# Another order of issue for the steps of a delta-rule attention and MLP-mixer kernel

## The chip, the cores and the metric

The kernel runs on one core of one Trainium2 chip. The metric is the device time of one execution in microseconds. Before the change the median of three runs is 701.34 us (700.79 to 702.61).

## What is computed

Two blocks follow each other. The first is a delta-rule recurrence over 768 positions for 4 batches of 8 heads of 48 features; the second is an MLP mixer on its output, 4 x 768 x 384, in float32:

```python
for t in range(S):
    kt, vt, bt = (k_n[:, :, t], v[:, :, t], beta[:, :, t, None])
    y[:, :, t] = np.einsum('bhd,bhde->bhe', q[:, :, t], state)
    v_old = np.einsum('bhde,bhd->bhe', state, kt)
    state = state + bt[:, :, :, None] * np.einsum('bhd,bhe->bhde', kt, vt - v_old)
...
xt = x.transpose(0, 2, 1)
h = np.maximum(xt @ w_tok1, 0.0) @ w_tok2
u = x + h.transpose(0, 2, 1)
h2 = np.maximum(u @ w_ch1, 0.0) @ w_ch2
return (u + h2).astype(np.float32)
```

k_n is k divided by its norm. The token weights are 768 x 256 and 256 x 768, the channel weights 384 x 1536 and 1536 x 384.

## The kernel before

The recurrence is computed in chunks of 64 positions, two to a unit u of 128; there are 24 units, six to a batch. Every piece of work is a Python generator, a job, that issues a few instructions and yields. One string, `order`, names the job whose next step is issued; "p0*3" means three steps of job p0. Nothing else sets the order. Each engine takes its instructions in the order in which the steps issue them, and the semaphores follow from the tiles that they share. So a step in the string stands at once in the queues of all the engines that it uses, and an instruction that waits holds those behind it on its engine.

The jobs, by the first letter of their names:

- k, v (lines 326 and 354): loads of k and q, and of v, for a unit, issued from SP's queue; v ends with a scaling on GpSimd.
- p (line 374): norms on ScalarE and VectorE, transposes of k and q into p_t and their copies, the product p_g of keys and queries (64x64 array tiles), its masking on VectorE (line 442), then the parts of the matrix that is to be inverted.
- i (line 531): the inversion of the unit triangular 32x32 blocks of a round of units, some thirty dependent pairs of VectorE instructions (lines 553 and 558). Rounds 0 and 1 (units 0 to 3, and 4 and 5) have a shorter way that works on 16x16 halves and stays in SBUF; later rounds go through DRAM (n_dram, w_dram).
- f, h, j (lines 514, 577 and 608): bring the inverses back, and join the halves with small matmuls (p_z and p_x, on 32x32 array tiles).
- r (lines 635 and 712): the recurrence, one step for each chunk of 64, 48 in all. Within a step of the first batch, VectorE subtracts (line 659), PE forms p_w, ScalarE copies it, PE forms p_s, and VectorE updates the state (line 688). The next chunk needs that state.
- m (line 880): the mixer of a batch: the token product p_1 (six steps), the second token product p_h (six steps, each added on VectorE), then the channel products p_c and p_o. From batch 1 on the channel products use seven products in the place of eight.
- w (lines 237 and 273): a piece of a weight matrix: a load, then rounding on ScalarE, VectorE and GpSimd. There are 34; s forms sums of weights, b loads beta.
- x, z, y and Y (lines 196 and 205): fillers. x multiplies a tile of zeros with itself, 128x128; z does so with 512 columns; y and Y issue four matmuls of 64x128. All write p_warm, which nothing reads, and wait for nothing but the zeros.

PE's matmuls in float32 show as two records each in the profile, transposes as one.

Of the kernel before, what the change touches and what calls it, by code (L numbers as in the profile page):

```python
# [23 lines left out]
def kernel(  # L24
# [1052 lines left out]
    r3*3 w14 p7 p8 p7 j2 p7 k10*2 r4*2 i1 v3 w9*2 p7*3 r4*3 i1 j3*2 v3 w9*2 r4 j3 i1
    j3 r4 w5*2 r2 r5 p6 r4*2 p6*2 w9 i1 p8 p6 k10*2 r5 w5*2 i1 p7*3 k11 v3 r5*3 p8*2
    w5 k10 k11 r5*3 p8*2 i1 p8*2 r5 v3*2 w16 v4 w16 r6*3 w16 w24*2 i1 w27 v4 p7 v4
    p7 h5*2 r6*2 w16 h4 w16 p7 r6*2 p8*2 w27 v4 w24 p9 h4 f4*4 r6*2 r7*2 p9 w24 w27  # L1080
    p9 p10 w24 p8 w27 p8*2 w27 r7*4 f5 p7 k12 w28*2 p9*7 w28 r7*3 v5*2 h4*4 w26 z
    w29 h4 p8 p9 v5*2 w26 f5*2 w26 f5 p9*2 r3 v4 w26 h5*2 z j4 h5*3 w28 k13 p8 w26
    w29 p8 j4*2 w29 r8 p8 w28 w29 k12 j4 v5 p9*2 j4 j5 r8 z p9 r8 p10*3 r8*2 p9 j5
    w7*3 w29 r8*3 i2*3 p10 j5*3 w7 r9*2 w15*2 i2 r9*3 k13 w7 w15*2 i2 r9*4 k12*2 w4
    i2 k12 w4 i2 r8 w4 w15 p12 r10*2 i2*2 w19*2 p10 k11*2 r10*4 i2 w19 v6 w4*2 k11*2
    r10*2 i2 w19*2 w22 k12 i2 r10 r11*3 m0 i2 r11*2 w22 i2 v6 m0 w12 k13*2 w12 i2
    w22 w31 i2 v6 i2*2 w12 i2*3 w12 v7 k13 v7*3 r11*2 i2*2 w12 i2 w21 w22*2 i2 w25
    i2 v6*2 i2*6 m0*2 p10*5 f6 m0*3 p12 m0 f6 m0 w27 m0*2 p10 m0 f6*2 w31 m0*2 f8
# [2 lines left out]
    f9*3 p10 k13 r12*2 w23*2 j7 m0 r12*2 j8 m0 j7*2 r13*2 m0 w23 p11 p12 p13 j8
    w32*2 p11 r13*2 w32 p11 m0 p13 r13*2 p13 w32*2 p11*4 m0 r14*2 p11 m0 w29*2 v8*2
    r14 w30 p11*2 j8 w23 w25 r14 p12 w30*2 r14 w23 r14 m0 w30 j8 w30 w25 k14 r15*2
    p13 p12 p11 p12*3 m0 v8*2 p12 v8 r15*2 p12 m0*2 w33*2 f9 p11*2 r15 p12*2 r15 w33
    m0 w29 p13*5 m0 p11 v9 w33 r16*2 j9 k14*4 k15 p12*4 p13*2 v9*2 p13*6 w33*2 m0*2
    w33*2 w31 v9 w31 j9 r16 p14*2 m0*3 r16*3 j9 p14 m0 w31 p14*2 r17*2 m0 v9 j9*2
    k14 i3 r17*2 i3*2 m0 i3 k15 v10 p14*4 k15 v10 i3 v10 i3 k16 v10 i3 k15*2 m0*2
    i3*2 r17*2 m0*2 r18 k15 i3*4 m0*3 i3 p14 r18 i3*3 k16*3 m0 i3*2 k16*2 i3*13
    r18*2 p15 p14*2 m0 p14*2 r18*2 m0*5 f10 v10 m0*7 f10*3 m0 r19 f11*2 r19 p14 p15
    f11 j10 m0 p15 m0*3 r19*2 j10*2 f13*4 f12 p15*2 m0 r19*2 j10 m0 p15 p16 f12 r20  # L1100
    v11 p14 f11 j10 p15*4 r20 m0 j11 f12 r20*2 k17*2 p15*2 k17 v11 f12 v11*3 p14
    p15*2 m0 p15 r20 p15 r20 j11 j12 m0 r21 j11*3 r21 j12 r21*2 m0 s*2 p16*5 j12 p16
    k17*2 v12 k18 m0 v12 m0 p17 j13 r21*2 p16*3 m0 r22 p17 r22 k18 k17 p17 v12 p16*4
    m0 s p17 r22*2 m0 r22 p16 r22 p16*2 m0 r23*2 p17*2 p15 m0*2 v13 m0*2 r23 p17*2
    m0 r23 v12 r23 v12 r23 k19 p17*3 m0*3 v13*2 k18*4 p17*5 m0*2 p17 j13 m0 j12 i4*2
    m0*3 i4*3 m0 i4 m0 i4 v13 m0*2 i4*2 k19 m0*2 k19*2 i4*2 m0 i4 p18 i4 m0*3 k19
    i4*2 j12 j13 m0 k19 j13 i4*2 r24*2 m1 i4 r24*3 m1*2 i4 r25 i4*2 p18*2 r25 i4*3
    v14*2 i4 j13 m1 i4 m1 r25 v13 m1 r25*3 m1 p18 r26*2 i4 m1 v14 i4 v14 i4 p18 i4
    p18 k20 r26 m1 i4*2 r26*3 m1 p19 v14 p18*4 m1 f14 s r27*2 p18*3 f14*2 k20*2 m1*3
    r27*2 p19*2 m1*2 j14 f15*2 f14 f16 f15*2 m1 r27*2 j14*2 m1*2 j15 r28*2 j14 f16  # L1110
    j14 j15*2 k20 f16 p18*2 m1 f17*2 k20 r28*2 p19 j16 m1 p20 r28 j16 r28 j15*2
    r29*2 p20 j16 m1 p19*4 r29 p19 k20 m1 p20 r29*2 p19 v15 p19 f17 r29 v15*4 m1*2
    r30*2 p18 f16 m1*4 r30*2 v16 k21 v16 p18 k21 p19 k21*3 p19 p21 m1 p21 m1*2 v16
    r30 v16*2 p20*4 r30 p20*3 m1 p21 k21 p19*3 r31*2 p20*2 k22*3 p20*3 f17 p20 m1*2
    k22 j16 k22 r31 m1*3 j16 r31 j17 m1 r31*2 v17*2 p20 p21*2 v17 p21*3 m1 r32*2 m1
    p21 m1*2 r32*2 p21 p19 k22 v17 p22 p21*3 p22*2 m1 r32*2 m1 p21*4 p22*2 m1*2
    r33*2 m1 j17 r33*2 k23 m1 k23 i5*3 v17 m1*2 i5*4 v18 k23*2 v18*3 r33 k23*2 r33
    p22 j17*3 i5 m1 p23 m1*3 i5*2 m1 i5 m1 i5 r34 i5*2 m1 r34 m1*7 r34*2 m1 i5 p22
    m1*4 i5 r34*2 m1 i5 m1 i5 m1*2 v18 p22 i5*3 m1*5 r35 m1*6 i5*3 m1*3 i5*2 m1 i5*2
    m1*2 i5*4 p23*2 m1 f18*3 r35 m1 f19 m1 p22*2 f19 f20 f19 f20*3 m1*2 r35*2 p22*3  # L1120
    m1*2 p23 j18 p23 p22*2 m1 p23 f18 m1*5 j18*2 m1*3 p23 m1*2 r35 j19*2 j18 p22 f19
    m1 v19*3 j19 m1*2 p22 m1*6 f21*4 m1*2 j18 m1 p23 m1*2 v19 m1*6 r35 r36*2 p23*4
    r36*3 m2 p23 j20 r37 j20 j19 v19 p23 r37*3 p23*3 v20 m2 j21 r37*2 j20 m2 v20 r38
    j19 m2 r38*2 i6 m2 r38 i6*5 r38*2 i6 m2 r39*2 j21 i6 v20 j20 i6*3 r39 i6 m2 j21
    i6 r39 m2 j20 r39*2 v21*2 m2 v21 m2 v21 m2 i6 v20*2 r40*2 m2*2 i6 m2*2 j21*2 r40
    m2 r40 i6*2 m2*2 r40 i6 r40 i6*2 m2*6 i6 m2*3 r41 m2*4 i6 r41 m2*2 r41*2 i6*5
    v21 m2*2 v22*5 r41*2 m2*5 r42*2 m2 i6*5 m2*3 r42 f22 m2*2 f22*3 f23*3 r42*3 m2*2
    j22 r43 m2 r43 m2*2 j22 j23 v23 j22 r43*2 v23*3 m2*2 r43*2 v23 j22*2 j23*2 f23
    m2 r44*2 m2*2 r44*2 m2*3 r44*2 m2*3 r45*2 m2 j23 m2*2 r45*2 m2*2 r45 j23 r45
    m2*3 r46*2 m2*4 r46 m2*2 r46 m2*3 r46 m2 r46 m2*2 r47 m2 r47 m2*2 r47 m2 r47  # L1130
# [38 lines left out]
```

## Time and profile before

| What | Value |
|---|---|
| median of three runs | 701.34 us |
| the profiled execution's own time | 703.88 us |
| its span, first to last instruction | 702.1 us |
| mean granted TensorE clock | 0.944 of full speed |
| TensorE clock at half speed, from that mean: 2 x (1 - 0.944) x 702 | 78.6 us |
| SP's DMA issues | 438 |
| fillers in the order: x, z, Y | 6, 9, 3 |

The span is that of the core's instructions in one profiled execution; its own time includes what lies around the span, here 1.8 us. Times below are counted from the start of the span. A busy share says little on its own here, since the early part (attention of the first batch, rounding of weights, inversions) and the late part (mixers) have different limits.

### The profile page before, as it was taken

To read this page: it belongs to the slowest core of one execution; us is meant where nothing else is said; L and a number is where in the kernel's file an instruction comes from. 1 tells how busy PE (TensorE), PEld (TensorE's weight loads), DVE (VectorE), ACT (ScalarE), POOL (GpSimd) and SP (SyncE) were. 2 spreads that over 40 slices of the span, in tenths; PEclk is the share of its full clock that TensorE was granted. 3 is DMA by queue.
4 is the path that set the end of the run, shared out by engine and by line. 5 is a ranking of instruction groups with operands and counts; after the bars stand their busy time and mean duration, and the time that the engine had idled before them with its cause. 6 is when DMAs were issued, how large, how long until landed. Compare 5 with 4: busy or idle time off the path is not lost.

```text
span 702.1 us, 18867 instructions
## 1 busy us (share of the span) xinstructions
PE 660.9 (94%) x7794; PEld 594.8 (85%) x7794; DVE 476.5 (68%) x1263; ACT 279.7 (40%) x659; POOL 105.9 (15%) x130
## 2 busy tenths in 40 slices
PE   8448988798999999999999999999999999999998
...
DVE  6998787898899955499577895358955533252433
...
PEclk9856689599999999999999999999999999999999
...
GB/s 183 168 91 112 112 142 149 166 85 110 65 95 111 60 63 74 86 38 62 76 70 94 41 1 95 8 56 15 13 54 14 1 23 1 22 2 23 1 23 23
DMA packets 146901, 46.15 MB, mean 66 GB/s; under 512 B 138080, under 2 KB 141280, under 8 KB 146816
## 3 DMA queue, kind: packets, MB, share of 16 engines
...
q8 instruction: 61, 1.00, 0.6%
q14 instruction: 24, 0.20, 0.1%
...
## 4 chain that ended last, share of the span: by engine, by line
PE 83%; DVE 11%; DMA 2%; issue 2%; ACT 2%; SPq 0%; ACTq 0%; DVEq 0%
PE p_o L992 24%; PE p_r L818 7%; PE p_c L973 7%; PE p_c L818 7%; PE p_d L818 5%; PE p_q L730 4%; PE p_s L756 4%; PE p_w L746 4%; PE p_h L900 3%; PE p L887 3%; PE p_g L436 3%; PE p_z L619 2%; PE p_x L628 2%; DVE sub L553 2%; DVE x L558 2%
## 5 line engine op out<-in xcount | busy, mean ns | idle before, releaser
L992 PE MATMUL p_o<-wc,r 128*128 128x192 f32 x720 | 126.0, 328 | 0.6 <-ACT u_t L914 0.6
L992 PEld LDWEIGHTS p_o<-wc,r 128*128 128x128 f32 x720 | 116.4, 190 | 1.8 <-ACT u_t L914 1.1
L918 DVE TENSOR_TENSOR xb<-xb,p_o 128x192 f32<-128x192 f32 x84 | 29.5, 352 | 57.0 <-PE p_o L992 56.6
L558 DVE TENSOR_TENSOR x<-x,sub 128x84 f32<-128x84 f32 (+24 forms) x178 | 59.8, 336 | 6.1
L553 DVE TENSOR_TENSOR sub<-x 128x84 f32<-128x84 f32 (+24 forms) x178 | 58.1, 326 | 7.6 <-DMA x<-n_dram 3.9
L973 PE MATMUL p_c<-u_t,wc 128*128 128x256 f32 x216 | 52.1, 392 | 0.0
L835 DVE TENSOR_TENSOR r<-p_r,r 128x384 f32<-128x384 f32 x36 | 20.0, 555 | 46.1 <-ACT r L864 35.6
L992 PE MATMUL p_o<-wc,s 128*128 128x192 f32 x288 | 50.7, 327 | 0.0
L264 POOL TENSOR_TENSOR w_f<-w_f,d 128x384 uint32<-128x384 uint32 (+1 forms) x34 | 34.2, 1008 | 94.9 <-DVE w_f L257 50.1
L838 ACT ACTIVATE r<-r 128x384 f32<-128x384 f32 x72 | 37.5, 524 | 23.6 <-DVE r L835 21.5
L992 PEld LDWEIGHTS p_o<-wc,s 128*128 128x128 f32 x288 | 46.8, 190 | 0.0
L749 ACT COPY rw_bd<-p_w 64x192 f32<-64x192 f32 x72 | 22.4, 311 | 59.1 <-PE p_w L746 53.6
L973 PEld LDWEIGHTS p_c<-u_t,wc 128*128 128x128 f32 x216 | 40.6, 194 | 5.8 <-issue 0.7
L818 PE MATMUL p_r<-u_t,wc 128*128 128x128 f32 x324 | 45.4, 276 | 0.0
L818 PE MATMUL p_c<-u_t,wc 128*128 128x128 f32 x324 | 45.2, 276 | 0.0
L358 POOL TENSOR_TENSOR v_st<-v_st,nrm 128x384 f32<-128x384 f32 x24 | 20.2, 845 | 165.3 <-DMA v_st<-in_v_dram 116.4
L818 PEld LDWEIGHTS p_r<-u_t,wc 128*128 128x128 f32 x324 | 40.8, 192 | 0.1
L818 PEld LDWEIGHTS p_c<-u_t,wc 128*128 128x128 f32 x324 | 40.5, 192 | 0.2 <-issue 0.2
L415 POOL TENSOR_TENSOR mb<-mask_c,cs 128x512 f32<-128x512 f32 x20 | 21.2, 1059 | 128.9 <-DVE cs L397 113.2
L436 PE MATMUL p_g<-kqt 64*64 64x128 f32 x704 | 29.4, 299 | 7.4 <-ACT kqt L425 5.9
L887 PE MATMUL p<-xb,w 128*128 128x384 f32 x96 | 35.5, 509 | 0.0
L730 PEld LDWEIGHTS p_q<-s_bd,kqt 128*128 128x128 f32 x264 | 33.3, 192 | 2.1 <-issue 0.5
...
## 6 DMA issues: line engine op xcount, KB each, us to landing
...
```

Of the source, the lines that this page charges most:

```text
L264: nc.gpsimd.tensor_tensor(out=f, in0=f, in1=lo, op=ALU.add)
L436: nc.tensor.matmul(p_g[cc][PAR[i ^ cc], p], kqt[PAR[i], 2 * p + cc, 0], kqt[PAR[i], 2 * p + cc],)
L553: nc.vector.tensor_tensor(out=tmp, in0=y[:, :, 0:s, s : s + 1].to_broadcast([n, k, s, w]), in1=y[:, :, s : s + 1, s + 1 : m].to_broadcast( ...
L558: nc.vector.tensor_tensor(out=y[:, :, 0:s, s + 1 : m], in0=y[:, :, 0:s, s + 1 : m], in1=tmp, op=ALU.add,)
L730: nc.tensor.matmul(p_q[:, p], kqt[:, 2 * p + cc], s0[:, p])
L746: nc.tensor.matmul(p_w[0 : C + 1, p], gm[:, 2 * p + cc, 0 : C + 1], r_bd[:, p])
L818: nc.tensor.matmul(p[:, i], weight(g * n + i), b_, start=first and i == 0, stop=True, skip_group_check=True,)
L838: nc.scalar.activation(out, out, ACTF.Relu)
L887: nc.tensor.matmul(p_1[dh], piece_of(w1, c, 0)[:, dh * 128 : (dh + 1) * 128], xb[:, c], start=(c == 0), stop=(c == NCH - 1),)
L918: nc.vector.tensor_tensor(out=xb[:, c, e], in0=xb[:, c, e], in1=p, op=ALU.add)
L973: nc.tensor.matmul(p_c[:, k], piece_of(wc1, cb, f * 128)[:, f * 128 : (f + 1) * 128], u_t[:, cb], start=(cb == 0), stop=(cb == NCB - 1),)
L992: nc.tensor.matmul(p, a[:, m], wc2[:, m, j], start=(start and m == 0), stop=(m == NM - 1), skip_group_check=True,)
```

## The change

Only the string is another one. It names the same steps of the same jobs, each as often as before, save for the fillers: x goes from 6 to 17, z from 9 to 21, Y from 3 to 11, and the string from 2142 steps to 2173. The order within a job can't change. Between jobs it changes nearly everywhere in the first half; the last 114 steps are those of m3 in both.

The lines of the diff that hold the beginning, the first joins and recurrence steps, and the first mixer:

```diff
-    w10 z x*2 w10*2 k0 x z b w2 w1 k0 w10 k0*3 w10 k0 x p0 w2*2 p0 b*2 p0 x k1 w2 w1
-    p0*3 w2 k2 p0 w1 k3 p0*2 k1 z p0*2 z k1*2 p0 w3 k2 k1*2 p1*2 p0 v0*2 k2 k4*2 k2
...
-    i0*4 v0 p4*2 i0*3 w18 i0*2 p4*2 w18 w6 w13 k8 p5 i0 h0*2 p6 h1 k8 h1 w6 p5 w6
-    f0*2 v0 v1 v0 p4 k7*2 f1 k7 f1*2 f0*2 f1 w13 h2*2 h0 k7*3 z p6 w18 w13 p6 h0*4
-    p7 j0*2 w8*2 h1 p5 w13*2 w8 f2*3 j0 h1*3 p7 w8 h1 Y j1 p6 w11*2 w8 w11 j0 p5 j0
-    p5*4 r0*2 w17 f2 w17 h2*2 r0 h2*3 w11 v1 w17 p7 p4*2 p5 r0 p5*3 v1*2 r1*2 k8 r0
...
-    w21*2 r12 v7 w21 Y w31 j6 w21 f7*3 w20 f7 f8*2 j6 w25*2 p10 j7 j6 w25*3 p11*2
-    w20*2 f8 w23 w31 w27 w20 w31 w27 w20 m0*2 j7 j6*2 w23*2 p11 p12 m0 p10*3 j8 m0*2
...
+    w10*5 Y x z k0 b w2 w1 x*4 Y k0*5 p0 w2*3 w1*2 k1 p0 w3 b*2 k2 k1 Y k3 p0 w2
+    p0*4 x p0*3 k1*4 p1 w3 p0*2 p1 p0 x k2*3 p1*5 k4 k2 k3 Y k4 Y k4 w3 p1*2 k4 k2
...
+    p4 i0*2 k5 v0 w1 p4*2 i0*3 w3 i0*3 p4*4 k6*2 k7 i0*2 w18 i0*2 k6*2 x p4 i0*2
+    k5*3 k6 k5 k7 w18 k6 k7 Y z k7*2 i0*2 v1 w6 v0 h1 p5 p4*2 w18 h0 w6 p5 w6*2 p6 z
+    i0 h0 p6 z p5 f1 h1 k8 w6 f0 w18 f0*2 v0 f0 p4 f1*3 k5 w13*2 h2 w13 f2*2 h2 h0*4
+    p7 h0 x z w8*2 j0 w8 p5 h1 w13 h1*2 w13 j0*2 p5 z f2*2 h1 w8 p6 j0*2 h1 p7 p5*4
+    h2 w8 w11 v1 h2 w11 r0*2 w11 h2*3 z r0 p5*2 w17*2 p6 p4*2 w17 r0 r1 w17 p5*3
...
+    v6 p10*5 x m0*3 w27*2 w31 m0 p12 m0 p12 m0*2 p10 m0 p11 m0 f6*3 f7 f6 w21 w25 f9
+    w21*2 m0 z w25 j6*2 f7 f8 f7 w21 w25 p10 w20 w31*3 r12 w25 j6 j7 w31 p12 w20*2
+    w25 f7 w25 p10 f8 w23 w20*2 m0*3 f9*2 j6 w23 j6 j7 w23 p10 m0*2 f8 p11 v7 w23
```

More of the change, by code (lines that the diff above doesn't have):

```diff
@@ L1064 @@
     order = """
-    w10 z x*2 w10*2 k0 x z b w2 w1 k0 w10 k0*3 w10 k0 x p0 w2*2 p0 b*2 p0 x k1 w2 w1
-    p0*3 w2 k2 p0 w1 k3 p0*2 k1 z p0*2 z k1*2 p0 w3 k2 k1*2 p1*2 p0 v0*2 k2 k4*2 k2
-    p1*2 k2*2 p1*6 k3 p2 w3 k3*2 p2 k3*2 k4*3 w3 p1*3 p2*3 p3*2 k6 p2 k5 p2*3 p3*3
-    p2*4 p0 p4*2 k5 p3*3 p1 p3*3 w1*2 p3 p2 p3 p1 p2*2 p0 p4 k4 p0 w3 p2 p3*3 p1*2
-    p4*2 p3 p0 k6*2 z w6 k6*2 p4*4 x i0 w3 i0 k6 w18 k5*4 p4 i0*3 w6 i0 w18 i0 p5
-    i0*4 v0 p4*2 i0*3 w18 i0*2 p4*2 w18 w6 w13 k8 p5 i0 h0*2 p6 h1 k8 h1 w6 p5 w6
@@ L1071 @@
-    f0*2 v0 v1 v0 p4 k7*2 f1 k7 f1*2 f0*2 f1 w13 h2*2 h0 k7*3 z p6 w18 w13 p6 h0*4
-    p7 j0*2 w8*2 h1 p5 w13*2 w8 f2*3 j0 h1*3 p7 w8 h1 Y j1 p6 w11*2 w8 w11 j0 p5 j0
-    p5*4 r0*2 w17 f2 w17 h2*2 r0 h2*3 w11 v1 w17 p7 p4*2 p5 r0 p5*3 v1*2 r1*2 k8 r0
-    Y w17*2 p5 w11 w14*2 r1 k8 r1 h3 p5*3 r1*2 r0 f3*2 j1*2 h3 f3 i1 r1*2 f3 v1 i1
-    k9*4 w0 v2*4 p6 w14 r2 i1 j2 p6*5 j1*2 r2 r1 i1 p7 r2*3 w0 j2*2 i1 w14 w0 r2 i1
-    h3*2 r2*2 w0 v2 h3*3 k9 k8 k9 i1 r3*2 k10 i1*2 p6*2 j3 i1 k8 p6 r3 w0 r3*2 j2
@@ L1077 @@
[L1077 to L1088, printed above, removed]
@@ L1089 @@
-    w21*2 r12 v7 w21 Y w31 j6 w21 f7*3 w20 f7 f8*2 j6 w25*2 p10 j7 j6 w25*3 p11*2
-    w20*2 f8 w23 w31 w27 w20 w31 w27 w20 m0*2 j7 j6*2 w23*2 p11 p12 m0 p10*3 j8 m0*2
[L1091 to L1130, printed above, removed]
@@ L1131 @@
-    m2*17 r47*2 m2*12 m3*13 m2 m3*2 m2*13 m3*114
+    w10*5 Y x z k0 b w2 w1 x*4 Y k0*5 p0 w2*3 w1*2 k1 p0 w3 b*2 k2 k1 Y k3 p0 w2
+    p0*4 x p0*3 k1*4 p1 w3 p0*2 p1 p0 x k2*3 p1*5 k4 k2 k3 Y k4 Y k4 w3 p1*2 k4 k2
+    p2 p1*2 k3 p2 v1 v0 p1 k3 p1 k3*2 p2*2 p3*2 p2*5 w3 p3*3 x Y z p0 p1 p2*4 p0 w1
+    z p3*5 Y p0*2 k4 p3 k4 p4*2 p3*2 p1*2 p2 x p4 p2*3 z*2 p3*2 v0 v1 w18 p3*2 p4 p1
+    p4 i0*2 k5 v0 w1 p4*2 i0*3 w3 i0*3 p4*4 k6*2 k7 i0*2 w18 i0*2 k6*2 x p4 i0*2
+    k5*3 k6 k5 k7 w18 k6 k7 Y z k7*2 i0*2 v1 w6 v0 h1 p5 p4*2 w18 h0 w6 p5 w6*2 p6 z
@@ new lines @@
+    i0 h0 p6 z p5 f1 h1 k8 w6 f0 w18 f0*2 v0 f0 p4 f1*3 k5 w13*2 h2 w13 f2*2 h2 h0*4
+    p7 h0 x z w8*2 j0 w8 p5 h1 w13 h1*2 w13 j0*2 p5 z f2*2 h1 w8 p6 j0*2 h1 p7 p5*4
+    h2 w8 w11 v1 h2 w11 r0*2 w11 h2*3 z r0 p5*2 w17*2 p6 p4*2 w17 r0 r1 w17 p5*3
+    k8*2 z v1 w17 p5*3 p6 r1 h3 j1 i1 r0 w14 w11 h3 w14 r1*2 k9 k8 r1 w11 w14 i1
+    j1*2 k9*3 r1*3 w0 k8 x p6*3 f3 p6 f3 p6 p7 j1*2 v2*3 i1 r2*2 z p7 i1 r2 w0 i1*2
+    j2 i1 f3*2 r2*5 h3*3 i1 Y w14 h3 r0 h3 r3*2 k9 i1 j2*2 p8 k9 w0 k8 k7 i1 p8 r3
@@ new lines @@
+    p6 k10*2 p6*2 r1 r3 w0*2 x r3*3 v2*2 j2*2 w14 r2 k10 p7*2 j3 r4*3 r3 i1 r4 w9 j3
+    w9 i1 w5 r4 k11 w9 p9 v3 p6 w16 j3 r4 i1 r4 p7*4 w9 j3*2 w5 i1 k10 w5*2 v3*2 r3
+    p9 p8 v3 i1 v3 p6 w9 p7*2 r5 p7 r4*2 r5*4 p8*2 w16 i1 w24 w5 p8*4 k10 r5*4 w24
+    w16 k11 w24 h5 k11*2 r6*4 h5 r6 z w27 i1 p7 v4 p6 w16*2 w24*2 h4*2 f4 w27 r6*3
+    v4*2 f4*3 p7 f5 p8 f5*2 w27 r7*2 p8 r7*2 p8*2 w27 w26*2 w27 p9 v4 w26 p9*2 r7*2
+    p9*3 p7*2 p9 w28*2 h4*5 w28 r7 p9*2 r7 z r8 z w26 p9*2 j4*2 v5 v4 p10*2 v5 r8
@@ new lines @@
+    p8*2 w28 r6 w28 p10 f5 p10 v5 Y w29*3 r8 w26 k11 j4*2 p8 p6 p8 v5*2 j4 w29 p9*2
+    h5*3 r8*2 z h5*2 p9*2 r8 w7 i2 w29 z w7*3 x r8 x j5 i2 r9 w7 r8 j5 i2 r7 r8 w4*2
+    i2*2 z w15 r9*3 p10 r9 k11 r9 w15 k10 k12 i2 w15 i2 r9*2 i2 w4 i2 r10*3 j5 w15
+    j5 Y i2 w19 w15 i2 k13 w19 k13 j5 i2 k13 w19 p10 w4 r10*4 z i2 w19*2 r9 i2 w4 i2
+    w12*2 i2 x m0*2 r10*2 k12 r11*3 v7*2 k12 i2 w22*2 k13 i2 k13 w22 m0 r11*2 k12*2
+    r11 i2 w12 i2 w25 i2*2 w12 r11 i2 w22*2 m0 i2 w21 v7 w12 v7 k12 i2*6 v6*4 i2*2
@@ new lines @@
+    v6 p10*5 x m0*3 w27*2 w31 m0 p12 m0 p12 m0*2 p10 m0 p11 m0 f6*3 f7 f6 w21 w25 f9
+    w21*2 m0 z w25 j6*2 f7 f8 f7 w21 w25 p10 w20 w31*3 r12 w25 j6 j7 w31 p12 w20*2
+    w25 f7 w25 p10 f8 w23 w20*2 m0*3 f9*2 j6 w23 j6 j7 w23 p10 m0*2 f8 p11 v7 w23
+    p10 r12*2 w27 j7 m0 r12 j8*2 w23 j7 p13 r12 w23 j9 j8 r13*2 w29 m0 j7 m0 r13*2
+    w32 f8 w32*2 m0 r13*2 v8 w32*2 v8 p11*6 p13 m0 r14*2 p11*4 w23 p11 w29 m0 r14
+    p13 r14 w30*4 j8 p12 p11 p12 r14*2 j8 w25 p10 k14 m0 p12*2 r15 p12*2 m0 k13 p12
@@ new lines @@
+    v8 r15*2 w30 p12 p13 m0*2 v8 p11*3 k14*2 w33 r15 p12 k14*2 r15 v10 p12 f9 p13*2
+    k14 r15 p13 m0*2 p12 p13 p12 p13 v8 p12*2 w33 w23 w33 r16 w33 r16 p13*4 w33 p14
+    m0 r16*2 v10*2 w31*2 p13*4 w31 w33*2 m0*2 j9 r16 w29 m0 r16 p14 m0*2 r17*2 p14*2
+    i3*2 j9 v9 m0*2 v10 j9*2 r17*2 p14 w33 i3*3 p14 i3*3 v9*2 m0 v9 r17*2 k15 m0 v9
+    m0 k15 m0 r18 i3 r18 i3 m0 k15*2 p14 k15*2 p14 i3*6 r18*2 m0 i3*6 p15 i3*6 k16
+    i3*4 m0 r18*2 m0 f13 m0 p14 f10*3 m0*13 p14*2 m0 r19*2 m0*2 p14*2 m0 f10 r19*2
@@ new lines @@
+    v10 j10 m0*2 p15 r19*2 p15 v11 f13 v11 f11*2 j10*2 p15*3 f12 r20*2 k16 f11 f12
+    f11 k16*4 j10*2 v11 f12 p15 f13 p15 f12 v11*2 p15 j11 m0 r20*2 p15*3 m0 r20*2
+    j11 m0 r21 p14 m0 k17 j11 p15 k17*2 j12 j11 p16 p15 j12*2 r21*2 p16*2 v12*2 k17
+    m0 p15 k17*2 p15 j13 m0 r21*2 j11 p16 r21 p16*2 m0 p15 p16*4 r22 m0 r22*2 p16
+    p14 p16 r22 p14 p16 p17*2 p16*3 v12 p14 v12*2 m0 f13 k18 r22*2 p17 m0 r23*2 m0
+    p17*6 r23 m0 p16 r23*2 p17 k18 p17*3 k18*3 r23 p17 s*2 p18 m0*3 p17*2 k18 p17 s
@@ new lines @@
+    m0*3 p18*2 m0*3 i4 j13 j12*2 i4*2 m0 i4 m0 i4 m0 i4 m0*2 j13 i4*2 m0 i4 m0*2 i4
+    m0 i4 v13*3 m0 v13 i4*4 m0 i4 m0 k19*3 i4 m0 i4 m0 j13 r24 j13 i4 r24*2 m1 r24*2
+    m1*2 i4*3 r25*2 i4*10 m1*2 v13 r25 m1 r25*3 m1*3 r26*2 p18*2 k19*2 p18 k19 m1
+    f15 p18*2 f14*2 r26*2 v14 f14 m1 r26*2 p19 p18 f14 p19 m1 r27*2 m1 v14 p18*2
+    v14*3 p18 f15 f16 f15 f16 j14 p18 f16 p18 m1*2 r27*2 p19 m1 j14 k20*2 f17 k20*2
+    j14 r27 m1 k20 f15 f17 r27 j15 m1*2 r28*2 v15*2 f17 v15*3 j14 p18 j14 p18 j15 m1
@@ new lines @@
+    r28 m1 r28*2 j16 s j16 r28 j15*3 j16 r29*2 m1 p19*2 f17 p20 r29*2 m1 r29*2 p19*4
+    m1 r30 v16*3 k20 v16 p19 p20 r30 k21*2 p19 m1 p19*2 p18 m1*3 r30*2 k21 p19 p20*3
+    k21 p20 m1 k21 m1 p20 j17 r30 p20 r30 m1*2 p20 r31*2 p21 p20*2 k21 p20*2 k22 m1
+    p20*3 m1 f16 k22*3 v17 k22*2 p19 p21 m1 p21 r31 m1 p21*6 r31 m1*3 v17 m1 r31*2
+    p21*4 k23*3 p21*3 p19*2 v16 m1*4 r32*2 j16*2 p20 j17 p22 m1 p22 v17 r32 p21 j17
+    m1*2 r32*3 k23 m1*2 r33*2 m1 j17 r33 i5*2 m1 i5 j17 i5*2 v17 i5*2 v17 m1*2 r33*3
@@ new lines @@
+    m1*2 p22 i5 m1*2 i5*2 v19*3 k23 p22*6 r34*2 m1*4 i5*2 p22 m1*3 r34*2 i5 p22*2
+    m1*5 p22 r34*2 p22*3 p23 m1*2 i5*2 m1*2 i5 m1*2 k23 i5*2 m1*4 r35 m1*7 r35 i5*2
+    m1 i5*2 m1*4 i5 p23 m1*3 i5*2 m1*6 i5*3 p23 i5*4 v19 m1*2 v18 m1*3 v18 f18 f21
+    r35 m1 f18 m1 f19 v18 m1*3 f19 p23 f19*2 m1*4 p23*3 m1 f20 p23 m1*2 p22 m1 f18*2
+    f21*2 v19 p23 v18 f20 r35*2 p23 v18 j18*3 m1*2 j19 m1*3 j19 j18*2 f20 m1*3 j20
+    m1 r35 j19 m1*2 r36*2 p23*2 r36*3 m2 r37 f20 p23*3 j20 p23 j19*2 p23 r37*3 m2
```

9 lines of the change are left out of this document (added).

## The prediction

> **What bounds the kernel now.** I read the page first (busy shares and the forty slices), then the busy times by stretches cut where the TensorE clock changes, then VectorE's waits, and last the timelines of three places. From the page:
>
> ```profile
> PE 660.9 (94%) x7794; PEld 594.8 (85%) x7794; DVE 476.5 (68%) x1263; ACT 279.7 (40%) x659; POOL 105.9 (15%) x130
> ...
> PE   8448988798999999999999999999999999999998
> ...
> DVE  6998787898899955499577895358955533252433
> ...
> PEclk9856689599999999999999999999999999999999
> ```
>
> The reader is to see two regimes. In the first ten slices (17.55 us each) VectorE is the fullest and PE's clock falls to half again and again; after that PE is full at full clock. By stretches (window, its length, then busy PE, PEld, DVE, ACT, POOL, the clock, DMA share, GB/s):
>
> ```profile
> 30.00:64.00 34.00, 19.90 (x622) 16.36 (x614) 30.54 (x81) 17.72 (x43) 14.05 (x17) 0.51 0.53 112
> ...
> 77.00:94.00 17.00, 17.00 (x355) 15.69 (x351) 11.68 (x36) 7.48 (x19) 3.66 (x4) 0.51 0.59 122
> ...
> 125.00:142.00 17.00, 13.31 (x176) 10.65 (x178) 15.36 (x48) 6.41 (x17) 2.96 (x3) 0.50 0.63 154
> ...
> 166.00:182.00 16.00, 16.00 (x205) 13.69 (x204) 12.84 (x31) 10.55 (x26) 4.37 (x4) 0.89 0.50 112
> 182.00:702.00 520.00, 516.52 (x4896) 482.10 (x4894) 323.98 (x855) 174.97 (x406) 42.72 (x49) 1.00 0.20 43
> ```
>
> From 182 us PE has work for 516.5 of 520 us at full clock; no order of the same work can shorten that much. All that an order can win lies before 182 us, where VectorE is busy for 152.5 us (the eight stretches up to there summed) and 23 of its idle 29.5 us lie in waits of over 0.15 us each. VectorE's waits in that stretch (first eight; waiter, released by, us in total, times, longest):
>
> ```profile
> DVE gm L604 <- ACT gm L604: 4.0, 8, 0.9
> DVE s_bd L688 <- PE p_s L684: 3.6, 3, 2.2
> DVE wc L266 <- ACT d L263: 2.2, 1, 2.2
> DVE wc L266 <- POOL w_f L264: 2.2, 3, 1.3
> DVE w_f L252 <- DMA d<-in_moe_w_ch_dram: 2.0, 1, 2.0
> DVE sub L553 <- DMA x<-n_dram: 1.9, 1, 1.9
> DVE wc L442 <- PE p_g L436: 1.7, 1, 1.7
> DVE rw_bd L659 <- issue: 1.4, 1, 1.4
> ```
>
> Those that come from PE I look up in the timeline (start, length, what; idle before in brackets). The first is behind a filler at half clock:
>
> ```profile
> 9.77 1.91 PE L200 MATMUL p_warm<-warm 128*128 128x512 f32 x2
> ...
> 10.01 0.58 ACT L425 COPY wc<-p_t 128x512 f32<-128x512 f32 x1 [0.36 <-PE p_t L422]
> ...
> 11.61 1.45 PE L436 MATMUL p_g<-wc 64*64 64x128 f32 x32
> ...
> 13.11 0.69 DVE L442 TENSOR_TENSOR wc<-p_g,mb 128x512 f32<-128x512 f32 x1 [1.66 <-PE p_g L436]
> ```
>
> The copy that p_g needs ends at 10.59; p_g starts at 11.61, behind the filler. The others are in the recurrence at half clock and just before the saturated part:
>
> ```profile
> 88.97 0.73 DVE L688 TENSOR_TENSOR s_bd<-s_bd,p_s 48x192 f32<-48x192 f32 x2 [2.25 <-PE p_s L684]
> ...
> 164.97 4.54 PE L973 MATMUL p_c<-u_t,wc 128*128 128x256 f32 x12
> ...
> 170.48 4.15 PE L973 MATMUL p_c<-u_t,wc 128*128 128x256 f32 x18
> ...
> 176.64 0.56 DVE L266 SCALAR_TENSOR_TENSOR wc<-d,w_f 128x384 f32<-128x384 f32 x1 [2.22 <-ACT d L263]
> ```
>
> Twelve p_c records cost 4.54 us from 165 and eighteen cost 4.15 from 170.5: at the later pace twelve take 2.77, so the half clock costs 1.8 there.
>
> **What the Trainium skill says.** "TensorE: Matmul & The Clock Gate", Part 1, says that PE starts at half clock, goes to full after about one busy window of 3.4 us and back after an idle one, and that the windows run free of the kernel's start. The trace agrees on the two values and the grain: the clock is at half for 78.6 us (2 x (1 - 0.944) x 702) in stretches of 3.4, 17.1 and 34.1 us. It does not agree that idleness alone lowers it: from 77 to 94 us PE is busy throughout and stays at half, mostly with bursts of 64 or 32 of the array's 128 rows. "TensorEngine Tiling (Array Packing)", Key Properties, says that a change of tiling mode drains the array. The trace shows it as about 0.1 us: a p_q burst takes 0.86 us before a full-width burst and 0.96 before a tiled one.
>
> **The change part by part.** The job steps are the same multiset but for fillers: x (128x128) goes from 6 to 17, z (128x512) from 9 to 21, Y (64x128, four matmuls) from 3 to 11. At full clock these are about 0.21, 1.0 and 0.26 us, at half clock twice that; together 11.0 us become 27.4. Nothing reads p_warm, so a filler costs only if a ready burst stands behind it on PE. Behind the first step of mixer(0) one filler is left in the old order and two in the new.
>
> Next I weigh what stands on each queue before a milestone, each instruction at its median from the trace. VectorE, before and after: first invert step 22.5 and 22.2 us; first join_16 burst 39.6 and 36.5; recur 0, 49.6 and 48.1; recur 5, 74.2 and 77.9; recur 8, 97.6 and 94.3; first p_1 matmul 114.8 and 117.9; the first p_h, 130.7 in both; m0's 23rd step (at 181.7 us in the trace) 151.1 and 151.3. ScalarE has 109.7 and 109.0 before that last milestone, GpSimd 62.5 in both. PE's own work without fillers is 88.3 and 87.8 us there, and 512.1 and 512.5 remain behind it. So the work is shuffled within the early stage and is level where PE saturates. The end moves by what the 23rd step of m0 moves.
>
> Tile-mode changes behind the first p_1 go from 85 to 82, counted both ways; at 0.1 us that is 0.3 at most, nothing. The last 114 steps are m3's in both, so the tail (last add and store, some 2.5 us) stays.
>
> First gap: in the new order one x, not a z, stands between p0's transposes and its p_g, and w3's first VectorE instruction moves ahead of p0's product. The wait of 1.66 should fall to about 0.2: -1.5, bounds 0 and -1.7.
>
> Recurrence 3 and 4: waits of 0.92, 1.38 and 2.25 us, all at half clock. Between VectorE's two instructions of a recur step the chain PE, ScalarE, PE takes 2.05 us at full clock (recur 6: 98.55 to 100.6) and 4.2 here. The cover on VectorE in recur 4 is 2.1 us in both orders. So the order alone does not help; the clock does. -4.6 if it is full, 0 if not; I take -2.5, as five z now stand between join_16(0) and recur 1 where one stood, plus two more around recur 2, and only an x and a Y between there and recur 4.
>
> The 162 to 177 us stretch: a z now stands ahead of the join burst j6 (PE idles 1.8 us there, so it is covered), which should hold the clock for p_c; and w23's ScalarE square is issued before recur 12's copies, not behind them, which takes the cause of the 2.22 wait. The two overlap in time: -2.0 together, bounds 0 and -2.2.
>
> The load of x for the third inversion (6.6 us, with 1.3 of a weight load's wait and 1.9 of its own left open) keeps its place: 6.3 us of VectorE work cover it in both orders, and on SP's queue p9's four writes and one w7 load stand ahead of it in both. Nothing. The waits on ScalarE at L604 (4.9 with the wc group) stay, perhaps -0.5: between h3's two copies 0.6 us of other work now stands. SP and GpSimd issue the same instructions; the loads moved (k, v, w) land in 2 to 4 us and are issued tens of steps ahead, so nothing.
>
> New cost: fillers in front of ready bursts. At full clock a z delays by at most 1.1 us (12.99, 1.12 long), mostly covered by VectorE work of 1.6 to 4.4 us between recur instructions. I take +1.0, bounds 0 and +5.2 (below).
>
> Sum: -1.5 - 2.5 - 2.0 + 1.0 = -5.0. The span of 702.1 becomes 697.1, the profiled execution's 703.88 becomes 698.9. That execution lies 2.5 above the median of 701.34; taking the change off the median gives 696.3 us.
>
> **The rivals.** (1) The clock holds from about 50 us on and every term reaches its end: -1.7 - 4.6 - 2.2 - 1.0 and no cost, -9.5: 691.8. For it: 16 us more of filler. Against: the recur 2 to 5 stretch gets few of them, and 17 us of unbroken bursts did not lift the clock before. (2) The clock is no better where it matters, and only the first gap closes: -1.5, 699.8. (3) Slower: the fillers displace real work at half clock. Place: from join_16(0)'s first burst (42.5 us) to recur 1 (61.7), 19.2 us in the trace, PE holds 8.8 us of work counted at full clock, 17.6 at half: it is nearly PE's own bound. The new order puts 12.2 us there, 24.4 at half, which is 5.2 more than the 19.2. It decides if the clock does not rise within the first two z there, since then PE, not VectorE, sets the pace: -1.5 + 5.2 = +3.7, 705.0. Against it: those two stand where PE was busy for only 1.33 of 3.4 us (44.4 to 47.8).
>
> **How the numbers follow.** Forecast 0.42, rival 1 0.18, rival 2 0.22, rival 3 0.18. A difference of about 0.3% (2.1 us) is what a measurement of this kernel tells from none: the limits are 699.2 and 703.4. Faster: 0.42 + 0.18 and 0.04 of rival 2 = 0.64. Same: 0.18. Slower: 0.18. The range, 690.5 to 702.5, takes in rivals 1 and 2 and leaves out most of rival 3 and a little of rival 1's far end.
>
> **What would show it.** PE's clock at half for under 60 us in all (78.6 before), and full in most of 50 to 125 us; no wait over 0.5 us at p0's first product; the waits at L688 and L659 under 2 us in sum (5.0 before); the first p_h and m0's 23rd step earlier by 4 to 6 us; the rest, from that step to the end, within 1 us of 520.4. I am wrong if PE shows idle time after 180 us, if the clock's stretches are as long as before, or if VectorE shows new waits on PE between 45 and 80 us.

## The result, and the profile after

The changed kernel takes 697.78 us (median of 20 runs, 694.67 to 701.48); the kernel before took 701.12 beside it (20 runs, 698.32 to 705.95). The ratio is 0.9943, with a 95% interval of 0.9926 to 0.9959: 3.3 us faster between the medians, 4.0 by the ratio. The prediction said 696.3, in a range of 690.5 to 702.5.

The profiled execution of after took 695.09 us (span 693.3), 8.8 us less than that of before (703.88). That pair overstates the change, since before's profiled run lies in the upper part of its runs and after's in the lower part of its own. So differences between the two traces tell where time went, not how much of it remains in the median.

The page of after, the same four lines as the prediction shows of before (busy times; then PE, VectorE and the TensorE clock in forty slices):

```profile
PE 663.1 (96%) x7904; PEld 589.5 (85%) x7904; DVE 477.4 (69%) x1263; ACT 279.1 (40%) x659; POOL 106.0 (15%) x130
...
PE   8759989899999999999999999999999999999998
...
DVE  7999997998889854797676886368854532252433
...
PEclk9959999999999999999999999999999999999999
```

On the clock line six of before's first ten slices lie below 9, of after's one. Counted from the mean clock, 2 x (1 - 0.983) x 693, PE ran at half clock for 24 us where it was 78.6. (Both leave out the first 5 us or so: the record of the clock begins with its first change, and what lies ahead of that counts as full.) PE has 110 records more, the fillers. By stretches (same columns as of before):

```profile
30.00:64.00 34.00, 22.61 (x627) 13.91 (x623) 30.88 (x82) 17.58 (x42) 13.50 (x17) 0.75 0.53 121
...
77.00:94.00 17.00, 15.23 (x490) 13.46 (x482) 16.30 (x47) 12.44 (x34) 8.74 (x10) 1.00 0.58 132
...
166.00:182.00 16.00, 16.00 (x225) 14.47 (x223) 14.55 (x39) 10.28 (x27) 3.87 (x4) 1.00 0.23 61
182.00:693.00 511.00, 507.29 (x4785) 474.27 (x4783) 315.69 (x834) 170.34 (x395) 39.59 (x46) 1.00 0.20 44
```

The reader is to see the second line. From 77 to 94 us PE was busy all the time at a clock of 0.51 and VectorE for 11.68 us; now the clock is full, PE gets 490 records done where it did 355 (not all the same ones), and VectorE is busy for 16.30 us. PE no longer sets the pace there. VectorE's waits up to 182 us (waiter, released by, us in total, times, longest):

```profile
DVE gm L604 <- ACT gm L604: 3.9, 7, 1.5
DVE w_f L252 <- DMA d<-in_moe_w_ch_dram: 2.4, 2, 2.1
...
DVE rw_bd L659 <- issue: 0.6, 1, 0.6
...
DVE rw_bd L659 <- PE p_k L655: 0.5, 1, 0.5
```

The waits at s_bd L688 (3.6 us), on ScalarE's square for w23 (2.2), on the load of x (1.9) and at p0's first product (1.7) are gone; those at L604 stay. All waits of VectorE over 0.15 us in this stretch come to 13.2 us, from 23.1.

Step by step (traces; start of the instruction named, after less before): VectorE's masking of p0's first product -1.6 us, start of the first inversion -1.2, first join product (p_z) -1.1, first product of recurrence 0 -0.3, p_k of recurrence 3 -0.9, p_k of recurrence 6 -5.0, third inversion -7.9, the addition of the first p_h -7.8, the 23rd step of m0 -9.1, last VectorE instruction -9.2. What comes behind the 23rd step takes as long as before, 517.3 us to that last instruction for 517.4. The same holds for all twelve traces whose order is not split at that step: 517.3 to 517.6, whatever the order and the fillers. So the start of the 23rd step tells the whole time, and all that differs between these kernels lies ahead of it.

### The profile page after: what moved, and what is told of

The parts are those of the page before. It is cut to its first block, busy times and chain, and to the rows that moved or that the text cites. A ratio compares the mean times of both kernels' runs of the same rounds, so it can differ in the third digit from the quotient of the medians.

```text
span 693.3 us, 19064 instructions
## 1 busy us (share of the span) xinstructions
PE 663.1 (96%) x7904; PEld 589.5 (85%) x7904; DVE 477.4 (69%) x1263; ACT 279.1 (40%) x659; POOL 106.0 (15%) x130
## 3 DMA queue, kind: packets, MB, share of 16 engines
q8 instruction: 62, 1.02, 0.6%
## 4 chain that ended last, share of the span: by engine, by line
PE 85%; ACT 4%; DVE 4%; DMA 3%; issue 2%; POOL 1%; SPq 0%; ACTq 0%; POOLq 0%; DVEq 0%
PE p_o L992 24%; PE p_r L818 7%; PE p_c L818 7%; PE p_c L973 6%; PE p_d L818 5%; PE p L887 5%; PE p_h L900 5%; PE p_q L730 4%; PE p_s L756 4%; PE p_w L746 4%; PE p_g L436 3%; PE p_warm L200 3%; DMA d<-in_moe_w_ch_dram 2%; PE p_z L619 2%; PE p_x L628 1%
## 5 line engine op out<-in xcount | busy, mean ns | idle before, releaser
L973 PE MATMUL p_c<-u_t,wc 128*128 128x256 f32 x216 | 50.2, 383 | 0.0
L442 DVE TENSOR_TENSOR gm<-p_g,mb 128x512 f32<-128x512 f32 x44 | 28.9, 683 | 12.5 <-PE p_g L436 12.2
L845 ACT COPY r<-p_c 128x384 f32<-128x384 f32 x18 | 8.6, 478 | 67.8 <-PE p_c L818 55.2
L200 PE MATMUL p_warm<-warm 128*128 128x512 f32 (+1 forms) x76 | 34.6, 569 | 0.4 <-issue 0.4
```

What stands on the lines that cost most here:

```text
L200: nc.tensor.matmul(p_warm[:, 0:m], zero, zero[:, None, :].to_broadcast([128, m, 128]))
L442: nc.vector.tensor_tensor(out=blocks(gm)[:, :, cc, 0 : 2 * C].rearrange("s p (two n) -> s p two n", two=2), in0=p_g[cc], in1=mb[:, :, cc, ...
L973: nc.tensor.matmul(p_c[:, k], piece_of(wc1, cb, f * 128)[:, f * 128 : (f + 1) * 128], u_t[:, cb], start=(cb == 0), stop=(cb == NCB - 1),)
```

## The experiments

All compare with runs of the kernel before on the same chip. The medians of these sets of before differ by up to 1.4 us, so small differences between two kernels are better read from the ratios. "Half clock" in the last column is 2 x (1 - granted clock) x span, the median over the runs. It leaves out the stretch ahead of the first recorded change of the clock: 4 to 7 us in the traces of kernels that begin with fillers, but 15.5 and 16.0 us in the two without any filler and 20.5 us in the one without early fillers. PE ran at half there too: in the last of these p0's first p_g takes 1.99 us, a later one at full clock 1.10. So these three stand some 10 to 15 us too low in the column.

A trace is one run and need not lie near its kernel's median. Two lie well above it: the trace without join fillers by 5.9 us (the slowest of its 14 runs), that of the second hybrid by 6.4. The trace without early fillers lies 3.2 us above its median, the changed kernel's 2.7 below.

| Kernel | median us | runs | ratio to before, 95% | half clock us |
|---|---|---|---|---|
| before (four sets) | 700.6 to 702.0 | 158 | 1 | 71 |
| after | 697.78 | 20 | 0.9943 (0.9926 to 0.9959) | 24 |
| old order, no fillers | 703.12 | 22 | 1.0025 (1.0007 to 1.0042) | 85 |
| new order, no fillers | 703.55 | 17 | 1.0041 (1.0018 to 1.0063) | 90 |
| old order, new fillers | 709.99 | 6 | 1.0142 (1.0107 to 1.0177) | 50 |
| new order, old fillers | 706.16 | 9 | 1.0071 (1.0034 to 1.0108) | 83 |
| old order, new fillers up to 100 us | 705.59 | 22 | 1.0055 (1.0035 to 1.0074) | 62 |
| first gap's z moved | 702.21 | 14 | 1.0013 (0.9989 to 1.0038) | 72 |
| new, then old from m0's 23rd step | 703.15 | 22 | 1.0023 (1.0003 to 1.0043) | 32 |
| old, then new from there | 702.69 | 19 | 1.0027 (1.0000 to 1.0053) | 76 |
| after without early fillers | 699.84 | 16 | 0.9984 (0.9961 to 1.0006) | 33 |
| after without join fillers | 699.52 | 14 | 0.9971 (0.9945 to 0.9998) | 44 |
| after without late fillers | 697.98 | 16 | 0.9954 (0.9936 to 0.9972) | 49 |
| after and eight z more | 697.89 | 9 | 0.9934 (0.9903 to 0.9965) | 14 |

### Order and fillers, crossed

The order of the real steps and the places of the fillers were separated: each order with its own fillers, with the other's (each put behind the same PE step as in its own order), and with none. The places near recurrence 8 are shown.

The old order with the new fillers, against before:

```diff
-    h4*4 w26 z w29 h4 p8 p9 v5*2
...
-    w29 r8 p8 w28 w29 k12 j4 v5 p9*2 j4 j5 r8 z p9 r8 p10*3 r8*2 p9 j5 w7*3 w29 r8*3
+    h4*4 w26 w29 h4 p8 p9 v5*2
...
+    w29 r8 z p8 w28 w29 k12 j4 v5 p9*2 j4 j5 r8 p9 r8 p10*3 r8 z r8 p9 j5 z w7*3 w29
+    r8 z x*2 r8*2
```

The new order with the old fillers, against after:

```diff
-    w28*2 h4*5 w28 r7 p9*2 r7 z r8 z w26 p9*2 j4*2
...
-    j4*2 p8 p6 p8 v5*2 j4 w29 p9*2 h5*3 r8*2 z h5*2
+    w28*2 h4 z h4*4 w28 r7 p9*2 r7 r8 w26 p9*2 j4*2
...
+    j4*2 z p8 p6 p8 v5*2 j4 w29 p9*2 h5 z h5*2 r8*2 h5*2
```

> The old order of the real steps, with the new order's 49 fillers, each set behind the same PE step as there. Theory 1 (the clock that the fillers hold brings the gain): the clock is at half for under 50 us and the time falls to 697.5 to 699, a ratio to before of 0.995 to 0.997. Theory 2 (the new order of the real steps brings it): no gain, 701 to 704, whatever the clock does, since 16 us more of fillers stand on PE.

> The new order of the real steps, with the old order's 18 fillers, each set behind the same PE step as there. Theory 1: the clock is at half for some 75 us as before and the time stays at 700 to 702. Theory 2: 697 to 698.5 as after the change, with the clock as before.

> The old order of the real steps without any filler (nothing of the result is left out, since nothing reads what fillers write). Theory 1: slower than before, 703 to 708, with the clock at half for 90 us or more. Theory 2: not slower, 699.5 to 701, since the filler that stands before p0's first product is gone.

> The new order of the real steps without any filler. Theory 1: slower than before, 702 to 707, as the old order without fillers. Theory 2: 696.5 to 698.5, as after the change.

Both crossings lie above what either theory expected. The two kernels without fillers came out as theory 1 had it, and there the orders agree (703.12 and 703.55). The old fillers in the old order bring it to about 701.3, the new ones in the new order to 697.8, and both crossings came out slower than no fillers at all, the one in the old order clearly, the other by 0.3% with intervals that overlap. So neither the order nor the fillers carry the gain by themselves; the same 49 fillers take 5.8 us off one order and add 6.9 to the other. Where they do harm is seen in the timeline of the old order with the new fillers (start, length, what; idle before in brackets):

```profile
123.61 2.07 PE L200 MATMUL p_warm<-warm 128*128 128x512 f32 x2
...
126.61 2.08 PE L200 MATMUL p_warm<-warm 128*128 128x512 f32 x2
...
128.62 0.88 PE L684 MATMUL p_s<-rw_bd,gm 64*48 64x48 f32 x16
129.43 2.67 PE L200 MATMUL p_warm<-warm 128*128 128x512 f32 x6
129.54 0.74 DVE L688 TENSOR_TENSOR s_bd<-s_bd,p_s 48x192 f32<-48x192 f32 x2 [4.59 <-PE p_s L684]
...
134.66 0.36 DVE L659 TENSOR_TENSOR rw_bd<-p_k,v_st 128x192 f32<-128x192 f32 x1 [3.43 <-PE p_k L655]
```

The copy that p_s needs ends at 124.04 us. Two z that fall between the steps of recurrence 8, with a p_z between them, stand in front of p_s at half clock, and VectorE waits 4.59 us; the next fillers stand in front of p_k, 3.43 us. The new order with the old fillers shows the same on the joins:

```profile
117.91 2.08 PE L200 MATMUL p_warm<-warm 128*128 128x512 f32 x2
...
119.91 0.72 PE L598 MATMUL p_x<-gm,r 32*16 32x16 f32 x64
120.56 2.08 PE L200 MATMUL p_warm<-warm 128*128 128x512 f32 x2
...
120.98 0.28 DVE L604 COPY gm<-p_x 16x128 f32<-16x128 f32 x1 [2.37 <-ACT gm L604]
...
124.47 0.30 DVE L604 COPY gm<-p_x 16x128 f32<-16x128 f32 x1 [3.20 <-ACT gm L604]
```

The view names ScalarE as releaser at L604. The first time ScalarE itself waited for p_x, which stood behind the first z; the second time its copy stood behind that of p_w, which it awaited for 2.82 us and which stood behind the second z.

One further kernel left out of the old order with the new fillers the 13 that stand behind 100 us:

```diff
-    w29 r8 z p8 w28 w29 k12 j4 v5 p9*2 j4 j5 r8 p9 r8 p10*3 r8 z r8 p9 j5 z w7*3 w29
-    r8 z x*2 r8*2
+    w29 r8 p8 w28 w29 k12 j4 v5 p9*2 j4 j5 r8 p9 r8 p10*3 r8*2 p9 j5 w7*3 w29 r8*3
```

> The old order with the new fillers as in f1_old_order_new_fill, but without the 13 of behind 100 us. In the new order those 13 made no difference (697.98 with them left out, 697.78 with them). Theory A (the crossing is slow mostly where they fall between the steps of recurrence 7, 8 and 10 in the old order): 6 us or more of the crossing's 9 go, to 701 to 704, and the waits at s_bd and rw_bd around 130 us (4.6 and 3.4) fall under 2 each. Theory B (the early and join fillers cost it: L604 waits and norms around 48 and 63 us): 706 or more.

It came out between the theories. The waits fell as theory A had it (2.5 us at s_bd L688, 1.0 at rw_bd L659, from 5.2 and 4.3), and the ratio went from 1.0142 to 1.0055, but not to the level without fillers. About half of the crossing's loss against before lies in the late fillers (4.1 of 9.1 us by the medians, 0.87 of 1.42% by the ratios); the rest stays with the other 36. In the new order the late fillers made no difference, as is seen below.

### Which fillers the new order lives on

Three groups were taken out of the changed kernel, one at a time: early (all 24 of the first 31 us), joins (7 from 42 to 63 us) and late (13 behind 100 us). The other five of the 49 stayed in all three. A place of each, in this order:

```diff
-    w10*5 Y x z k0 b w2 w1 x*4 Y k0*5
+    w10*5 k0 b w2 w1 k0*5
...
-    h0 w6 p5 w6*2 p6 z i0 h0 p6 z p5 f1
+    h0 w6 p5 w6*2 p6 i0 h0 p6 p5 f1
...
-    r7 p9*2 r7 z r8 z w26
+    r7 p9*2 r7 r8 w26
```

> The new order without its 24 fillers of the first 31 us (10 x, 6 z, 8 Y, about 10 us of PE work at full clock). Theory A (they pay by the clock: without any filler the same order started the inversion 1.6 us later, at 29.78 for 28.14): i0 and h0 about 1.6 us later, all of it kept to the end, 699.4. Theory B (a delay that early is taken up while the inversion sets the pace): i0 later, r1 within 0.3 us, median within 0.1% of 697.8.

> The new order without the six z and one x that stand between 42 and 63 us, in the first joins and ahead of recurrence step 1. Theory A (my prediction's step: they raise the clock for recurrence steps 2 to 5): the clock stays at half until about 80 us as without any filler, r3 is 3 us and r6 4 to 5 us later, median 701 to 704. Theory B (the slower rival of the prediction: they displace ready joins at half clock): r1 0.5 to 1.5 us earlier and the end with it, 696 to 697.

> The new order without its 13 fillers behind 100 us (7 z, 4 x, 2 Y, about 8.4 us of PE work at full clock). Theory A (they hold the clock for recurrence 8 to 11, the token products and the third joins): the same to 106 us, then half clock in 20 us more and the end 1 to 2 us later, 699 to 700. Theory B (VectorE's other work covers PE there at half clock too): within 0.1% of 697.8. Theory C (they stand in front of ready bursts): up to 1 us faster.

Early: theory A by its number. The inversion starts 1.8 us later, the first join 1.8, and the median is 2.1 higher. Whether it is that delay that arrives is not shown: in this trace it is 3.1 us at recurrence 1 and 8.0 at m0's 23rd step, and later stretches at half clock can have their part in that. Joins: theory A in kind, by the traces. The stretches of 42 to 84 us, without them and then in the changed kernel, show it:

```profile
42.00:84.00 42.00, 35.80 (x1000) 30.59 (x992) 34.22 (x86) 27.26 (x66) 18.11 (x20) 0.50 0.48 100
```

```profile
42.00:84.00 42.00, 39.24 (x1170) 28.93 (x1163) 38.63 (x101) 30.83 (x77) 19.97 (x23) 0.87 0.52 114
```

Without them the clock stays at half for the whole 42 us, VectorE gets 86 instructions done for 101, and recurrence 3 and 6 start 4.9 and 6.0 us later than in the changed kernel. But these two traces are the slowest of 14 runs, with 62 us at half clock where the median is 44, and one of the fastest of 20. In the median 1.7 us arrive, less than expected, and the intervals of the ratios overlap slightly. So the direction is likely and the size is open. Recurrence 1 is only 0.25 us earlier without them: in these two traces displacing ready joins, theory B, costs that much and no more.

Late: theory B. The two stretches, without and with them:

```profile
107.00:138.00 31.00, 25.81 (x478) 21.80 (x480) 25.67 (x72) 15.71 (x40) 9.79 (x11) 0.56 0.66 147
```

```profile
107.00:138.00 31.00, 28.50 (x530) 19.10 (x529) 26.81 (x77) 13.68 (x36) 6.93 (x8) 0.94 0.65 151
```

The clock is at half nearly throughout instead of full, VectorE does 72 instructions for 77, and the median moves by 0.2 us (the ratio by 0.1%, within the intervals). Thirteen fillers hold the clock here for 25 us and buy nothing that can be measured. The run shows this sum only, not its two parts: the half clock may cost little there, or the fillers may cost what the clock brings.

### The first gap alone

```diff
-    k1 z p0*2 z k1*2
+    k1 p0*2 z*2 k1*2
```

> The order of before with one filler z (128x512) moved: it stood between unit 0's transposes and p0's first product p_g, and now stands behind that product. My prediction took this gap at -1.5 us (0 to -1.7) and carried it to the end. Theory A (the term stands: VectorE is the fullest engine early, so what it gains there arrives): m0's 23rd step and the end 1.5 us earlier, median about 699.5, ratio 0.998. Theory B (the gain is taken back by the next thing that is late, PE at half clock in the joins): the wait at L442 falls from 1.7 to under 0.3, r1 starts less than 0.5 us earlier, and the median stays within 0.1% of before.

Theory B by its outcome, but not by its path. The wait fell from 1.7 only to 0.9, since the clock was at half from 10.2 to 13.6 us in that run and p_g itself took 1.98 us (1.10 at full clock); the inversion started 0.2 us later than before, and the median did not move (1.0013, 0.9989 to 1.0038). The second hybrid below shows by chance what sets this gap. It has the instructions of before up to 182 us, that z in its old place among them, and in its profiled run:

```profile
9.26 1.02 PE L200 MATMUL p_warm<-warm 128*128 128x512 f32 x2
...
10.21 1.10 PE L436 MATMUL p_g<-wc 64*64 64x128 f32 x32
...
11.35 0.69 DVE L442 TENSOR_TENSOR wc<-p_g,mb 128x512 f32<-128x512 f32 x1
```

At full clock the z takes 1.02 us, p_g starts 0.1 us behind the end of the copy that it needs, and there is no wait. The two kernels without any filler, at half clock there, wait 1.4 and 1.8 us. So the gap of 1.66 us in before's trace comes and goes with the clock; at half clock the filler does delay p_g (it starts 1.0 us behind the end of the copy in before's trace, 0.05 with the z moved), but what the move won did not reach the inversion.

### Where in the order it lies

Two hybrids, split behind the 23rd step of m0, where PE saturates; behind it come the steps that are left, in the other order. New, then old, against after:

```diff
     m0 r13*2 w32 f8 w32*2 m0
-    r13*2 v8 w32*2 v8 p11*6 p13 m0 r14*2
+    p11 p10 k13 p11 p12 p11*2 p13 r13*2 p13 w32*2 p11*4 m0 r14*2
```

Old, then new, against before:

```diff
     m0 w23 p11 p12 p13 j8 w32*2 p11 r13*2 w32 p11 m0
-    p13 r13*2 p13 w32*2 p11*4 m0 r14*2
+    w25 j9 w29 r13*2 v8 w32*2 v8 p11*2 p13 m0 r14*2
```

> The new order up to and with the 23rd step of m0 (about 173 us), then what is left in the order of before. If all of the change lies in the early part (theory A): as the changed kernel, 697.8, ratio 0.9955 within 0.15%. If the saturated part also gained from its new order, or is tuned to it (theory B): 1 us or more slower than the changed kernel.

> The order of before up to and with the 23rd step of m0 (about 182 us), then what is left in the new order. Theory A (only the early part matters): as before, 700.9, within 0.15%. Theory B: 1 us or more off, in either direction.

The first came out as theory B's number, 703.15, more than 5 us above the changed kernel. Its trace shows why. Up to the 23rd step it is as early as after or earlier (171.46 us, after 172.60), and then it loses 6.3 us up to recurrence 16, at the seam (PE's timeline):

```profile
174.43 1.46 PE L973 MATMUL p_c<-u_t,wc 128*128 128x256 f32 x6
178.65 1.99 PE L730 MATMUL p_q<-s_bd,kqt 128*128 128x96 f32 x8 [2.76 <-DVE s_bd L764]
180.57 1.99 PE L436 MATMUL p_g<-kqt 64*64 64x128 f32 x32
182.49 2.87 PE L973 MATMUL p_c<-u_t,wc 128*128 128x256 f32 x6
```

In the hybrid p11, p10, p12 and p13 come before recurrence 13's next steps. PE waits 2.76 us for the state's update, which is queued on VectorE behind the norms of two units; the clock falls to half for the next two windows of 3.4 us, and a p_c burst takes 2.87 us for 1.46. The wait and half of 6.8 us at half clock make 6.2 of the 6.3 us, an estimate from these lines. Behind recurrence 16 another 0.3 us is lost at most. So the changed kernel's gain is there at the 23rd step, as theory A has it, and of theory B the second reason holds in a narrow sense: the first 25 us behind the seam must fit what stands ahead of it. The second hybrid is 0.27% slower than before (0 to 0.53), at the edge of what can be told from nothing; in its trace 0.9 us is lost behind the seam. Neither half of the order is better by itself.

### Eight more fillers where PE is idle

```diff
-    k7 w18 k6 k7 Y z k7*2 i0*2
+    k7 w18 k6 k7 Y z*9 k7*2 i0*2
```

> The new order with eight more fillers z in a row where PE has nothing to do during the inversion of units 0 to 3 (about 31 to 41 us), so that the clock should not fall to half for the stretch 36 to 53 us. Theory A (what is lost between 36 and 53 us in the changed kernel is lost to the half clock: two z at 2.8 and 1.9 us ahead of h2, joins at half speed): full clock in that stretch, h0 to r1 1 to 2 us earlier, and part of it at the end: 696.0 to 697.5. Theory B (the inversion on VectorE sets the pace there and the joins' delay is taken up later): no change from the changed kernel within 0.15%. Theory C (the eight reach into ready bursts of the joins): 1 to 3 us slower than the changed kernel.

Theory B. The clock between 40 and 60 us rose from 0.68 to 0.83 and the half-clock time fell from 24 to 14 us, but VectorE's busy time there is 17.9 us of 20 for 17.8; it sets the pace. The median is the changed kernel's (697.89). No kernel here is clearly faster than the changed one.

## Why the prediction came out

The direction and the place held: the gain lies ahead of m0's 23rd step, and the rest is as long as before. That it comes by the clock fits every trace and the crossed kernels, but order and fillers bring it only together, which the prediction did not have. The signs named in advance were seen: under 60 us at half clock (24), no wait over 0.5 at p0's product, waits at L688 and L659 under 2 us in sum (1.1), the rest within 1 us (520.7 for 520.4). No new wait of VectorE on PE stands between 45 and 80 us. The first p_h and the 23rd step came 7.8 and 9.1 us earlier in the trace, more than the 4 to 6 said, because the traces' pair is wider than the medians'. By terms:

- **First gap, -1.5.** The wait is gone and the first product 1.6 us earlier, but the reason given, the filler's place, does not hold: moving it alone gave nothing, and at full clock it costs nothing where it is. What closed the gap is the full clock, from 5 us on in after's trace. That the number came out is luck in part. That an early delay is carried to the end is likely and not shown: from the inversion (-1.2) the lead fell to 0.3 us at recurrence 0 before it grew again.
- **Recurrence 3 and 4, -2.5, "the order alone does not help; the clock does".** The first half is shown: without fillers both orders take the same time. For the second, the trace without join fillers stays at half clock and gets 86 VectorE instructions done for 101. From recurrence 3 to 6 the trace of after gained 4.1 us, close to the upper end, -4.6; how much of that is in the median is open.
- **162 to 177 us, -2.0.** The p_c bursts run at full clock and the square's wait is gone; between the transposes ahead of p_c (p_ut, at 161 us before) and the 23rd step the trace gains 1.5 us (-7.6 to -9.1). About right. The square's wait does follow the order: five of the six traces with the old order in this stretch have it (2.2 us in four, 1.3 in one), none of the eight with the new one. The clock's share has no run of its own.
- **The load of x, "Nothing".** Half right. VectorE's waits are gone in the trace, 3.2 us (1.3 for a weight load, 1.9 for x), but the load still sets the start of the third inversion: it lands at 125.43 us before and 117.49 after, and the inversion's first VectorE instruction on it starts within 0.03 us of that both times. From recurrence 6 to there the lead grows from 5.0 to 7.9 us. Most of that stands ahead of the load: the masking of p9, whose writes the load waits for, is 6.9 us earlier, the load's issue 7.3, and the load took 6.0 us for 6.6. Three of the six traces with the old order show a wait on x, none of the eight with the new one; no run isolates it.
- **L604, -0.5.** The wc and gm waits went from 4.9 to 4.7: nothing.
- **Fillers' cost, +1.0, bounds 0 and +5.2.** No run measures this term by itself. Over the 158 runs of before the time rises by 0.215 us for each microsecond at half clock (correlation 0.80), over the 20 of after by 0.207. With 0.21 for both, an estimate, the step from 71 to 24 us at half clock is worth 47 x 0.21 = 9.9 us; 3.3 to 4 arrived, so the added fillers would cost about 6. The prediction's gains summed to 6.0: the clock would be worth about 4 us more and the fillers cost 5 more, two errors that nearly cancel. But the rate is an average over places: eight more z took away 10 us at half clock where PE has nothing to do, and gained nothing; without the late fillers 25 us of half clock came back and cost nothing. If half clock is cheap in such places, the fillers cost less than 6, and the prediction's +1.0 may be right. Which it is stays open. One price was too low: at full clock a second Y adds 0.44 us in after's trace (1.09 for two at 12.28 us, 0.65 for one), not 0.26; for eight more that is 1.4 us of PE.

The same estimate, with the same doubt, orders the crossings. In the new order all 49 fillers take away 77 us of half clock (66 in the table, and 11 at the start that it leaves out), 16 us of gain; 5.8 are measured, so 10 of cost. In the old order they take away 46 us, 9.6 of gain, and 6.9 of loss are measured, so 16 of cost. That the order decides what the fillers are worth is shown without the estimate (5.8 us won, 6.9 lost, and no difference without any); the prediction, which priced order and fillers apart, has no term for that. The slower rival named the right mechanism, z in front of ready bursts at half clock, but at the joins: there two z take 2.8 and 1.9 us at half clock (43.2 and 45.8 us) and the clock rises at 53 us, so by the traces it cost 0.25 us at recurrence 1 instead of 5.2. It decided in the crossed kernels.

"TensorE: Matmul & The Clock Gate", Part 1 of the Trainium skill, says that the clock goes back to half after an idle window and that the windows run free of the kernel's start. The seam goes further than the first: the window of 3.4 us that holds the wait was not idle, PE was busy for 0.28 of it, and the next two still ran at 0.5. (The 17 us of busy PE at half clock, which the prediction sets against the page's idle window, speak rather against its other half, that a busy window brings the clock back.) With the second the traces agree: in the eleven that begin with fillers PE's first matmul starts at 1.05 or 1.06 us and the clock first rises between 4.3 and 6.8 us.
